# First stretch on six PSUM banks, units 8 to 11 later, units 10 and 11 in split precision, key tails over 128 rows

## The chip, the cores and the metric

The kernel runs on one core of a Trainium2 chip. The metric is the device time of one execution in microseconds (us). Short names: PE is TensorE (PEld its weight loads), DVE is VectorE, ACT is ScalarE, POOL is GpSimd, SP is the queue that issues most DMAs.

## The reference

Three layers follow each other on 2304 tokens: a linear attention with random features, a gated feed-forward layer, and a soft mixture of experts. Cut to what matters:

```python
# attention: q, k, v of shape (4, 8, 576, 64), omega (128, 64)
def phi(x):
    h = einsum('bhsd,md->bhsm', x, omega) - sum(x * x, -1) / 2
    return exp(h - max(h, -1)) / sqrt(128)
q_p, k_p = phi(q * scale), phi(k * scale)
kv = einsum('bhsm,bhsd->bhmd', k_p, v)
num = einsum('bhsm,bhmd->bhsd', q_p, kv)
den = einsum('bhsm,bhm->bhs', q_p, sum(k_p, 2))[..., None] + 1e-06
x = num / den                                   # then (2304, 512)
# gated layer: d_ff 1536
x = (1 / (1 + exp(-(x @ w_gate))) * (x @ w_val)) @ w_out
# soft mixture: 32 slots, 8 experts, softmax over tokens and over slots
logits = x @ phi2
slots = softmax(logits, 0).T @ x
slot_out = [relu(slots[e] @ w1[e]) @ w2[e] for e in range(8)]
out = softmax(logits, 1) @ slot_out
```

## The kernel before, in words

**Attention** works in 16 units, each two heads of one batch entry (`NU`). A unit has the steps `chunk_proj` (five, the products of keys and queries with omega, 9 tiles of 128 rows in all), `chunk_kv` (for each head five accumulating products over the 576 keys: four tiles of 128 rows and a tail of 64), `chunk_qT` (transposes) and `chunk_num` (numerator and denominator, two halves). The tail of 64 key rows shares a tile with the 64 tail rows of the queries: rows 0 to 63 of `HT` are keys, rows 64 to 127 queries. Four units make up one batch entry, and a block of the gated layer needs the four units of its tokens.

**Precision.** A product in plain fp32 is one call that PE runs as two instructions. Units from `N_PROJ` on (projection) and from `N_NUM` on (numerator) use the split form instead: each operand is cut into a high and a low part of type fp32r, and `three` issues three products of one instruction each. The gated layer always uses the split form.

**The gated layer** ("moe" in the code) walks five blocks of up to 512 tokens in 60 steps of one weight tile each: `gate(i)` (12 instructions into bank `ga`), `val(i)` (12 into `va`), `down(i - 1)` (12 into `o0` to `o3`). For the first steps the weights are also decoded from their stored form (`convert`, DVE and ACT work, staged in `g0`) and written to a scratch tensor `wscr`. The groups of steps are: block 0's first six weight tiles, block 1's twelve, block 0's last six, then blocks 2, 3, 4. Block 0's first part is set aside in `part`, and added back by `evac_out(0)` when group 2 (counted from 0) has ended.

**The order** of all instructions is made when the program is built: every step is recorded with a due time, and a list scheduler with its own cost table (`Plan`) writes out one fixed sequence for each engine. `LATE8` and the numbers `start`, `SPAN` set due times; no due time is a time on the chip.

**PSUM** has eight banks: `fl` (two), `ga`, `va`, `o0` to `o3`. While `wide[0]` is true (before the first gated step's due time) attention goes round the list `FLW`; afterwards it has the two `fl` alone.

**SBUF regions** `g0` to `g4` are reused: `split_regions` takes `g0` and `g1` over for the split operands (`XK`, `XQ` are the split keys and queries, `QT`, `KV` the split transposed queries and kv, `obh`, `obl` the split omega). `g0` holds the weight staging before, `g1` holds `part`. At the end all regions take the experts' weights.

Every recorded operation is issued by one line (L379), so the rows of the trace are told apart by tiles: `fl<-g,g` is an attention product into bank `fl`, `ga<-XT,w`, `va<-XT,w` and `o<-gt,w` are the gated layer, `x2T`, `x` and `ws` are weight decoding and staging.

Of the kernel before, what the change touches and what calls it, by code (L numbers as in the profile page):

```python
# [11 lines left out]
F32 = mybir.dt.float32  # L12
F32R = mybir.dt.float32r
# [7 lines left out]
B, H, S, D, M = 4, 8, 576, 64, 128  # L21
NU = B * H // 2
NT = 5
ROWS = [128, 128, 128, 128, 64]
DM, DFF, NTOK = 512, 1536, 2304
NF = DFF // 128

# [27 lines left out]
W1N = 6  # L55
W2N = 3
T0 = -60
N_PROJ = 12
N_NUM = 12
FLOOR = 8  # L60
EARLY = 12.0
SQP = [0, 0, 1, 1, 1, 0, 1, 0]
# [11 lines left out]
SPAN = [88.0, 115.0, 60.0, 120.0, 105.0, 45.0]  # L74
# [307 lines left out]
def body(ctx, tc, nc, qkT, tok, von, omT, wall, phi, w1, w2, ident_d, srep_d, rrep_d, mask_d, out):  # L382
    plan = Plan(nc)
    PE, ACT, DVE, POOL, SP = (Eng(plan, e) for e in ("PE", "ACT", "DVE", "POOL", "SP"))
# [6 lines left out]
    def T(shape, tag, dtype=F32, bufs=1):  # L391
        return plan.tile(sb, shape, dtype, tag, bufs)
# [46 lines left out]
    def region(k, dtype):  # L439
        return T([128, 4096], f"g{k}", dtype)  # L440

    def carve(reg, at, shape):
        n = int(np.prod(shape))
        names = "abcde"[:len(shape)]
        v = reg[:, at:at + n]
        if len(shape) == 1:
            return v
        return v.rearrange(f"p ({' '.join(names)}) -> p {' '.join(names)}",
                           **{c: d for c, d in zip(names, shape)})

    q0, q1 = (region(k, F32) for k in range(2))
    g2, g3, g4 = (region(k, F32) for k in (2, 3, 4))
    QS = [carve(q0, 1024 * k, [1024]) for k in range(4)]
    part = carve(q1, 0, [4, 512])
# [2 lines left out]
    def split_regions():  # L457

        nonlocal QT, KV, XK, XQ, obh, obl
        g0, g1 = (region(k, F32R) for k in range(2))  # L460
        QT = carve(g0, 0, [2, 2, S])
        KV = carve(g0, 2304, [2, 2, 128])
        obh = carve(g0, 2816, [256])
        obl = carve(g0, 3072, [256])
        XK = carve(g1, 0, [2, 640])
        XQ = carve(g1, 1280, [2, 512])
        hi_of(obh, obf, ("DVE",))
        lo_of(obl, obf, obh, ("DVE",))

# [2 lines left out]
    Vs = [carve(g3, 1280 * k, [NT, 2, 128]) for k in range(2)]  # L472
    QTF = carve(g3, 2560, [2, S])
    obf = carve(g3, 3712, [256])
    HK = carve(g4, 0, [4, 2, M])
    HQ = carve(g4, 1024, [4, 2, M])
    HT = carve(g4, 2048, [1, 2, M])
# [10 lines left out]
        return lst[ring[name] % len(lst)]  # L488

    wide = [True]  # L490
    FLW = ["fl", "o0", "o1", "fl", "o2", "o3", "ga", "va"]

    def bank(tag=None):
        if tag is None:
# [11 lines left out]
    def prep_qk(u, kind):  # L506

        if u >= NU:
            return
        if u == N_PROJ and kind == 0:  # L510
            split_regions()
# [37 lines left out]
    def chunk_kv(u):  # L549

        ps = bank()[:, 0:256].rearrange("p (h c) -> p h c", h=2)
        for h in range(2):
            for t in range(NT):
                k = HK[:, t, h, :] if t < 4 else HT[0:64, 0, h, :]
                PE.matmul(ps[:, h, :], k, Vs[u % 2][0:ROWS[t], t, h, :], start=t == 0, stop=t == NT - 1)
        if u < N_NUM:
            ACT.activation(out=KVF, in_=ps, func=AF.Copy, scale=1.0 / M)
            return
        ACT.activation(out=KV[:, 0], in_=ps, func=AF.Copy, scale=1.0 / M)
        DVE.scalar_tensor_tensor(out=KV[:, 1], in0=ps, scalar=1.0 / M, in1=KV[:, 0].bitcast(F32),  # L560
                                 op0=ALU.mult, op1=ALU.subtract)
# [314 lines left out]
    free, spare = [], []  # L876

    def pieces(tag, bufs=1, n=4):
        t = T([128, 1024 * n], tag, F32, bufs)
        return [t[:, 1024 * c:1024 * c + 1024] for c in range(n)]  # L880

# [208 lines left out]
    start = START  # L1090
# [68 lines left out]
    for g, (j, f0, f1) in enumerate(GROUPS):  # L1159
        span = SPAN[g]  # L1160
        for f in range(f0, f1):
            jobs += moe_jobs(i, start + span * (f - f0) / (f1 - f0), span / (f1 - f0))
            i += 1
        units, a0, a1 = {0: (range(4, 8), LATE0 + 5 * LATE1, start + 0.92 * span),
                         1: (range(8, 12), start, start + span + 0.9 * SPAN[2]),
                         3: (range(12, 16), start, start + 0.92 * span)}.get(g, ((), 0, 0))
        att = [c for u in units for c in step_chunks(u)]
        jobs += [(a0 + (a1 - a0) * k / len(att), "att", c) for k, c in enumerate(att)]
        if g > 1:
            m2c = moe2_chunks(GROUPS[g - 1][0])  # L1170
            jobs += [(start + span / (f1 - f0) + span * 0.7 * k / len(m2c), "m2", c) for k, c in enumerate(m2c)]
        if j == NB - 3:
            jobs += [(start + 10.0, "ex", load_w1)]
        if j == NB - 2:
            jobs += [(start + 10.0 + 12 * k, "ex", load_w1) for k in range(6)]
        if j == NB - 1:
            jobs += [(start + 10.0, "ex", load_w1), (start + EARLY, "end", free_early)]
        start += span
# [34 lines left out]
def layout(q, k, v, omega, moe_w_gate, moe_w_val, moe_w_out, moe2_phi, moe2_w1, moe2_w2):  # L1213
    def headsT(x):
        return x.reshape(B, H // 2, 2, S, D).transpose(0, 1, 2, 4, 3).reshape(NU, 128, S)

    def tiles(x, n):
        return x.reshape(NU, 2, n, 128, D).transpose(0, 3, 2, 1, 4)

    def pairs(x):  # L1220
        return x.reshape(NU, 2, S, D)

    kT, qT = headsT(k), headsT(q)
    kp, qp, vp = pairs(k), pairs(q), pairs(v)
    tail = np.concatenate([kp[:, :, 512:], qp[:, :, 512:]], axis=2)
    vtail = tiles(np.concatenate([vp, np.zeros_like(vp[:, :, :64])], axis=2), NT)
    ones = np.ones_like(vtail[:, :, :, 0])

    def up(w):
        return w.reshape(4, 128, NF, 128).transpose(2, 1, 0, 3).reshape(NF, 128, 512)  # L1230

    f32 = np.float32
    p = np.arange(128)
    big = np.finfo(f32).max
    a = {
        "qkT": np.concatenate([kT, qT[:, :, 512:], qT[:, :, :512]], axis=2),
        "tok": np.concatenate([tiles(kp[:, :, :512], 4), tiles(tail, 1), tiles(qp[:, :, :512], 4)], axis=2),
        "von": np.stack([np.concatenate([vtail[:, :, :, 0], ones], axis=3),
                         np.concatenate([ones, vtail[:, :, :, 1]], axis=3)], axis=3),
        "omT": np.concatenate([omega.T, omega.T], axis=0),  # L1240
        "wall": np.stack([up(moe_w_gate), up(moe_w_val), moe_w_out.reshape(NF, 128, DM)], axis=1).view(np.int64),
        "phi": moe2_phi.reshape(4, 128, NSLOT).transpose(1, 0, 2),
        "w1": moe2_w1.reshape(E, 4, 128, F).transpose(0, 2, 1, 3).reshape(E, 128, 4 * F),
        "w2": moe2_w2.reshape(E, 8, 128, 2, DM // 2).transpose(0, 3, 2, 1, 4).reshape(E, 2, 128, 4 * DM),
        "ident": np.eye(128, dtype=f32),
        "srep": (p[:, None] % 32 == np.arange(32)[None, :]).astype(f32),
        "rrep": (p[:, None] % 32 == p[None, :] % 32).astype(f32),
        "mask": np.where((p[:, None] % 32) // SPE == np.arange(E)[None, :], big, f32(0)).astype(f32),
    }
    return {f"in_{n}": np.ascontiguousarray(x) for n, x in a.items()}  # L1250
# [17 lines left out]
```

## Time and profile before

| what | value |
|---|---|
| time, median of 3 runs (lowest, highest) | 712.02 us (711.65, 712.44) |
| the profiled execution's own time | 711.95 us |
| its span, first to last instruction | 710.1 us |
| mean granted TensorE clock | 0.996 |
| PE busy | 690.2 us, 97% of the span |
| PEld, DVE, ACT, POOL busy | 77%, 62%, 61%, 41% |

The profiled execution is 0.07 us below the median, and 1.85 us of its time lie outside the span. A matmul's record is longer than the distance to the next one, since matmuls overlap in the pipeline; what an instruction costs the engine is read from start to start.

### The profile page before, as it was taken

How to read it: one execution, taken by the hardware profiler on the slowest of the kernel's cores; microseconds unless marked ns; L12 is line 12 of the kernel's file. 1: busy time of each engine (PE TensorE's matmuls, PEld its weight loads, DVE VectorE, ACT ScalarE, POOL GpSimd, SP SyncE). 2: the span in 40 equal slices, each digit the busy share in tenths (PEclk: the TensorE clock that was granted, in tenths of full speed). 3: DMA queues.
4: the chain of work that ended last, by engine and by line, in shares of the span. 5: the costliest groups of instructions: out<-in, count | busy, mean ns of one | idle time of the engine just before them, and what ended most of it. 6: DMA issues, size and time to landing. Idle time of an engine off the chain costs nothing.

```text
span 710.1 us, 11979 instructions
## 1 busy us (share of the span) xinstructions
PE 690.2 (97%) x4085; PEld 546.6 (77%) x4085; DVE 441.9 (62%) x1283; ACT 436.1 (61%) x976; POOL 291.2 (41%) x249
## 2 busy tenths in 40 slices
PE   8999999999999999999999999999999999999993
PEld 5667677768788787787788888788888788998662
DVE  4778998788998445463486765546554434775321
ACT  5889898889876644645467675654444445765021
POOL 0355344535445534435364553334444444642000
PEclk9999999999999999999999999999999999999998
DMA  8768777678784334622254234378633327657997
GB/s 296 278 220 285 264 246 262 216 250 283 250 295 138 122 122 136 226 79 68 77 168 137 83 93 161 99 270 298 236 95 94 101 83 247 198 165 208 338 408 263
DMA packets 49980, 139.47 MB, mean 196 GB/s; under 512 B 5504, under 2 KB 10880, under 8 KB 49920
## 3 DMA queue, kind: packets, MB, share of 16 engines
q1 hardware_dynamic: 45312, 121.94, 51.2%
q10 hardware_dynamic: 4608, 16.78, 6.8%
q8 instruction: 32, 0.52, 0.3%
q14 instruction: 28, 0.23, 0.1%
HBM read 124.54 MB, written 14.16 MB: 195 GB/s over the span
## 4 chain that ended last, share of the span: by engine, by line
PE 81%; DVE 3%; issue 1%; ACT 1%; DMA 1%; POOL 0%; POOLq 0%; ACTq 0%; DVEq 0%
PE o L379 23%; PE va L379 21%; PE ga L379 20%; PE fl L379 18%; DVE x2T L379 1%; DVE g L379 1%; DMA wscr<-x 1%; DVE x L379 0%; DVE gt L379 0%; POOL w L379 0%; ACT XT L379 0%; DVE ga_a L379 0%; ACT x2T L379 0%; POOLq L1257 0%; POOL x L379 0%
## 5 line engine op out<-in xcount | busy, mean ns | idle before, releaser
L379 POOL TENSOR_TENSOR w<-ws,w 128x512 fp32r<-128x512 f32 x138 | 182.9, 1326 | 238.0 <-ACT w L379 131.3
L379 PE MATMUL o<-gt,w 128*128 128x512 f32 (+1 forms) x720 | 169.0, 377 | 0.9 <-ACT w L379 0.8
L379 PE MATMUL ga<-XT,w 128*128 128x512 f32 (+1 forms) x720 | 167.1, 376 | 0.0
L379 PE MATMUL va<-XT,w 128*128 128x512 f32 (+1 forms) x720 | 166.5, 375 | 0.0
L379 PEld LDWEIGHTS va<-XT,w 128*128 128x128 f32 x720 | 124.4, 189 | 26.2 <-issue 4.5
L379 PEld LDWEIGHTS o<-gt,w 128*128 128x128 f32 x720 | 123.2, 189 | 27.2 <-issue 4.1
L379 PEld LDWEIGHTS ga<-XT,w 128*128 128x128 f32 x720 | 124.3, 189 | 25.7 <-issue 2.8
L379 ACT ACTIVATE g<-g 128x128 f32<-128x128 f32 (+3 forms) x339 | 119.2, 412 | 21.2 <-DVE g L379 9.5
L379 PE MATMUL fl<-g,g 128*128 128x256 f32 (+3 forms) x668 | 124.7, 345 | 4.1 <-DVE g L379 1.9
L379 PEld LDWEIGHTS fl<-g,g 128*128 128x128 f32 (+2 forms) x668 | 85.9, 178 | 32.4 <-issue 9.0
L379 ACT ACTIVATE w<-ws 128x512 fp32r<-128x512 f32 x107 | 67.3, 629 | 66.3 <-PE o L379 23.6
L379 ACT ACTIVATE ga_a<-ga 128x512 f32<-128x512 f32 (+1 forms) x60 | 33.3, 555 | 79.2 <-PE ga L379 79.1
L379 ACT ACTIVATE ga_a<-ga_a 128x512 f32<-128x512 f32 (+1 forms) x120 | 69.9, 583 | 10.6 <-DVE ga_a L379 9.6
L379 DVE CAST w<-ws 128x512 fp32r<-128x512 f32 x55 | 24.6, 448 | 78.9 <-PE ga L379 55.0
L379 DVE CUSTOM_DVE_ANT_0 g<-fl,g 128x128 f32<-128x128 f32 x252 | 59.0, 285 | 20.2 <-PE fl L379 17.5
L379 DVE SCALAR_TENSOR_TENSOR ga_a<-ga,ga_a 128x512 f32<-128x512 f32 (+1 forms) x60 | 38.1, 635 | 44.4 <-ACT ga_a L379 44.1
L379 DVE TENSOR_TENSOR ga_a<-va,ga_a 128x512 f32<-128x512 f32 (+1 forms) x60 | 38.1, 635 | 19.3 <-ACT ga_a L379 12.4
L379 POOL TENSOR_TENSOR XT<-g,XT 128x64 fp32r<-128x64 f32 (+2 forms) x45 | 29.1, 658 | 49.8 <-ACT XT L379 44.3
L379 ACT ACTIVATE x2T<-g 128x512 f32<-128x512 f32 x72 | 46.2, 667 | 2.6 <-DVE x L379 2.4
L379 DVE TENSOR_SCALAR x2T<-x2T 128x512 f32<-128x512 f32 x72 | 42.4, 597 | 1.1 <-ACT x2T L379 0.9
L379 ACT ACTIVATE ga_a<-ga_a,one_b 128x512 f32<-128x512 f32 (+1 forms) x60 | 40.7, 678 | 1.3
L379 DVE TENSOR_TENSOR gt<-ga_a,gt 128x512 fp32r<-128x512 f32 (+1 forms) x49 | 35.9, 732 | 1.4 <-ACT gt L379 0.4
(197 smaller groups left out, 683.5 us busy)
## 6 DMA issues: line engine op xcount, KB each, us to landing
ws<-wscr SPq DMA_DIRECT2D x42, 512.0 KB, 3.7
ws<-wscr SPq DMA_DIRECT2D x78, 256.0 KB, 2.7
g<-in_wall SPq DMA_DIRECT2D x36, 512.0 KB, 4.9
g<-in_von SPq DMA_DIRECT2D x16, 640.0 KB, 5.5
g<-in_w ACTq DMA_DIRECT2D x20, 512.0 KB, 5.0
wscr<-x SPq DMA_DIRECT2D x36, 256.0 KB, 4.4
g<-in_qkT SPq DMA_DIRECT2D x15, 576.0 KB, 3.8
g<-in_tok SPq DMA_DIRECT2D x15, 576.0 KB, 4.9
```

What stands on the lines that cost most here:

```text
L379: getattr(self.eng[e], method)(*a, **k)
```

## The change

It does five things. (1) `FLW` loses `ga` and `va`: in the first stretch attention goes round six banks. (2) `N_PROJ` and `N_NUM` go from 12 to 10: units 10 and 11 use the split form. (3) For that, the split regions must come earlier: `g1` is cut into two halves, `g1a` for `part` and `g1b` for `XQ`, `obh`, `obl`, and `XK` moves to the end of `g0`. (4) Units 8 to 11 get due times that begin 0.3 of group 1's span later (`LATE8`). (5) The key tail is multiplied over all 128 rows of `HT`; the values' rows 64 to 127 of that tile are zeros already, and the column of ones is zeroed there on the host.

```diff
-ROWS = [128, 128, 128, 128, 64]
...
-N_PROJ = 12
-N_NUM = 12
+N_PROJ = 10
+N_NUM = 10
+LATE8 = 0.3
...
+    def half_region(k, dtype):
+        return T([128, 2048], f"g1{'ab'[k]}", dtype)
...
-    q0, q1 = (region(k, F32) for k in range(2))
+    q0, q1 = region(0, F32), half_region(0, F32)
...
-        g0, g1 = (region(k, F32R) for k in range(2))
+        g0, g1 = region(0, F32R), half_region(1, F32R)
         QT = carve(g0, 0, [2, 2, S])
         KV = carve(g0, 2304, [2, 2, 128])
-        obh = carve(g0, 2816, [256])
-        obl = carve(g0, 3072, [256])
-        XK = carve(g1, 0, [2, 640])
-        XQ = carve(g1, 1280, [2, 512])
+        XK = carve(g0, 2816, [2, 640])
+        XQ = carve(g1, 0, [2, 512])
+        obh = carve(g1, 1024, [256])
+        obl = carve(g1, 1280, [256])
...
-    FLW = ["fl", "o0", "o1", "fl", "o2", "o3", "ga", "va"]
+    FLW = ["fl", "o0", "o1", "fl", "o2", "o3"]
...
-                k = HK[:, t, h, :] if t < 4 else HT[0:64, 0, h, :]
-                PE.matmul(ps[:, h, :], k, Vs[u % 2][0:ROWS[t], t, h, :], start=t == 0, stop=t == NT - 1)
+                k = HK[:, t, h, :] if t < 4 else HT[:, 0, h, :]
+                PE.matmul(ps[:, h, :], k, Vs[u % 2][:, t, h, :], start=t == 0, stop=t == NT - 1)
...
+        if tag == "g1":
+            halves = [half_region(k, F32) for k in range(2)]
+            return [halves[c // 2][:, 1024 * (c % 2):1024 * (c % 2) + 1024] for c in range(n)]
...
-                         1: (range(8, 12), start, start + span + 0.9 * SPAN[2]),
+                         1: (range(8, 12), start + LATE8 * span, start + span + 0.9 * SPAN[2]),
...
+    ones[:, 64:, NT - 1] = 0.0
```

Three places show how the order moves. The first is PE in the first stretch. `fl_...`, `o0_...` with `g3_78,g2_77` are projections (fp32), with `64x288` numerators, with `128x128` kv; `ga_145` is the gated layer's very first product. Before, units 3 and 4's work stands ahead of `ga_145`:

```order
L379 MATMUL fl_142<-g3_78,g2_77 128x256
L379 MATMUL o0_133<-g3_78,g4_79 64x288 x2
L379 MATMUL o1_134<-g3_78,g4_79 64x288
L379 MATMUL fl_132<-g3_78,g4_79 64x288 x2
L379 MATMUL o1_134<-g3_78,g4_79 64x288
L379 MATMUL ga_145<-XT_96,w0_138 128x512 x2
L379 MATMUL fl_135<-g3_78,g4_79 64x288 x2
L379 MATMUL fl_143<-g3_78,g2_77 128x256 x2
L379 MATMUL ga_145<-XT_96,w0_138 128x512 x3
```

In the change the same product begins at unit 1's numerators (`o2_112`, `o3_113`), two units earlier, and stands piece by piece between attention's steps:

```order
L379 MATMUL o1_110<-g3_78,g4_79 64x288 x2
L379 MATMUL o2_112<-g3_78,g4_79 64x288 x2
L379 MATMUL o3_113<-g3_78,g4_79 64x288 x2
L379 MATMUL ga_145<-XT_96,w0_138 128x512
L379 MATMUL o2_118<-g3_78,g2_77 128x256 x2
L379 MATMUL ga_145<-XT_96,w0_138 128x512 x2
L379 MATMUL o0_109<-g3_78,g4_79 64x288 x2
L379 MATMUL o0_115<-g3_78,g4_79 128x128 x2
L379 MATMUL fl_111<-g3_78,g2_77 128x256 x2
```

So the first weight tile's 24 products of gate and value are spread over units 1 to 4, and the same attention instructions stand around them.

The second place is PE at unit 10's first projections, in the change. `fl_316` is unit 9's kv, `ga_313` and `va_317` a gated step of block 1, `fl_320` the split projection (six instructions, two tiles of three); unit 10 had the fp32 form (two instructions, `g3_78,g2_77`) before:

```order
L379 MATMUL o3_260<-gt_293,w2_296 128x512 x3
L379 MATMUL fl_316<-g3_78,g4_79 128x128 x10
L379 MATMUL ga_313<-XT_164,w0_302 128x512 x12
L379 MATMUL fl_320<-g1b_312,g0_311 128x256 x6
L379 MATMUL va_317<-XT_164,w1_306 128x512 x12
```

The split keys (`g0_311`) must be written before `fl_320`, and they lie where the weights were staged.

The third place is PE around the end of block 0 (`XT_96`) and the start of block 2 (`XT_278` before, `XT_299` in the change). Before, unit 12's projections stand after the second gated step of the new block has begun, twelve in a row:

```order
L379 MATMUL ga_461<-XT_278,w0_451 128x512 x9
L379 MATMUL fl_394<-g0_380,g1_381 128x256 x2
L379 MATMUL fl_409<-g0_380,g1_381 128x256 x2
L379 MATMUL ga_461<-XT_278,w0_451 128x512 x3
L379 MATMUL fl_394<-g0_380,g1_381 128x256 x4
L379 MATMUL fl_409<-g0_380,g1_381 128x256 x4
L379 MATMUL va_470<-XT_278,w1_456 128x512 x5
```

In the change all five of unit 12's projection steps stand ahead of block 0's last products, its kv (`fl_452`) stands ahead of block 2's first product, and `fl_453` is unit 13's first projection:

```order
L379 MATMUL o3_395<-gt_434,w2_437 128x512 x3
L379 MATMUL fl_452<-g3_78,g4_79 128x128 x10
L379 MATMUL ga_449<-XT_299,w0_443 128x512 x12
L379 MATMUL fl_453<-g1b_312,g0_311 128x256 x6
L379 MATMUL va_454<-XT_299,w1_447 128x512 x12
```

So unit 12 no longer waits for `part`, which shared a region with the split operands.

## Rows read from the trace of the kernel before

**Rows 1.** The page: busy time of each engine, and the granted clock in tenths.

```profile
PE 690.2 (97%) x4085; PEld 546.6 (77%) x4085; DVE 441.9 (62%) x1283; ACT 436.1 (61%) x976; POOL 291.2 (41%) x249
...
PEclk9999999999999999999999999999999999999998
```

**Rows 2.** Busy time of each engine by stretch; then granted clock, DMA share, GB/s.

```profile
0.00:10.00 10.00, 6.84 (x23) 4.88 (x24) 2.68 (x15) 2.62 (x4) 0.20 (x4) 1.00 0.67 222
10.00:60.00 50.00, 48.17 (x267) 33.66 (x266) 36.89 (x199) 44.29 (x135) 19.06 (x22) 1.00 0.75 272
60.00:160.00 100.00, 99.48 (x493) 72.34 (x492) 87.88 (x272) 88.20 (x213) 42.45 (x39) 1.00 0.74 254
160.00:220.00 60.00, 59.40 (x281) 47.27 (x280) 54.87 (x128) 51.32 (x108) 31.34 (x24) 1.00 0.76 257
220.00:340.00 120.00, 120.00 (x601) 92.82 (x600) 60.35 (x155) 62.51 (x129) 53.80 (x45) 1.00 0.39 127
```

**Rows 3.** PE's waits between 10 and 640 us: us in total, times, longest.

```profile
PE fl L379 <- DVE g L379: 1.8, 4, 0.7
PE o L379 <- DVE g L379: 1.2, 2, 0.7
```

**Rows 4.** PE's instructions in order of time, 11 to 16 us: start, duration, count.

```profile
11.78 1.03 PE L379 MATMUL fl<-g,g 128*128 128x256 f32 x4
12.65 2.97 PE L379 MATMUL o<-g,g 128*128 128x128 f32 x20
15.55 0.66 PE L379 MATMUL va<-ident,g 128*128 128x128 f32 x4
```

**Rows 5.** The same, cut to the first six and eight of unit 3's kv.

```profile
46.93 0.83 PE L379 MATMUL o<-g,g 128*128 128x128 f32 x6
...
46.93 1.05 PE L379 MATMUL o<-g,g 128*128 128x128 f32 x8
```

**Rows 6.** Two gated products after a kv, and two not after one.

```profile
203.11 0.73 PE L379 MATMUL va<-XT,w 128*128 128x512 f32 x2
...
87.26 0.62 PE L379 MATMUL va<-XT,w 128*128 128x512 f32 x2
```

**Rows 7.** PE in order of time: fp32 numerators (128x288) between gated products.

```profile
85.39 0.50 PE L379 MATMUL va<-XT,w 128*128 128x512 f32 x1
85.72 0.40 PE L379 MATMUL o<-gt,w 128*128 128x512 f32 x1
86.05 0.71 PE L379 MATMUL fl<-g,g 128*64 128x288 f32 x4
86.68 0.73 PE L379 MATMUL o<-gt,w 128*128 128x512 f32 x2
```

**Rows 8.** The same for a split unit: projections (128x256) and numerators (128x288).

```profile
444.88 0.52 PE L379 MATMUL fl<-g,g 128*128 128x256 f32 x3
445.23 2.91 PE L379 MATMUL ga<-XT,w 128*128 128x512 f32 x12
447.98 0.95 PE L379 MATMUL fl<-g 128*128 128x288 f32 x6
448.77 2.90 PE L379 MATMUL va<-XT,w 128*128 128x512 f32 x12
```

**Rows 9.** PE and DVE at unit 12's first projections, in order of time.

```profile
359.12 1.21 PE L379 MATMUL fl<-g,g 128*128 128x256 f32 x8 [0.67 <-DVE g L379]
...
358.25 1.42 DVE L379 TENSOR_TENSOR g<-g,g 128x640 fp32r<-128x640 f32 x2
```

**Rows 10.** The splits of a split unit, 340 to 480 us: busy us, mean ns.

```profile
L379 DVE TENSOR_TENSOR g<-fl,g 128x512 fp32r<-128x512 f32 x8 | 5.5, 689 | 2.1 <-ACT g L379 1.9
...
L379 POOL TENSOR_TENSOR g<-g,g 128x640 fp32r<-128x640 f32 x3 | 4.9, 1640 | 5.2 <-ACT g L379 3.2 <-DVE g L379 2.0
```

**Rows 11.** Bank ga between 10 and 21 us: a projection's products and its readers.

```profile
L379 PE MATMUL ga<-g,g x7: 379/379/483, 10.8 to 21.0; 128*128 128x256 f32 x7
L379 DVE CUSTOM_DVE_ANT_0 g<-ga,g x4: 281/287/293, 18.4 to 19.6; 128x128 f32<-128x128 f32 x4
```

## The prediction

> **What bounds the kernel now.** I read the busy shares first, then the stretches, then PE's waits. PE is busy for 97% of the span and no other engine for more than 77%, which is PE's own weight loads [rows 1]. By stretch [rows 2] PE has 48.17 of 50 us from 10 to 60, 99.48 of 100 up to 160 and 120 of 120 from 220 to 340; what idle time it has lies at the two ends. In the whole middle its two longest entries of waiting, both for DVE, come to 3.0 us [rows 3]. So the time is PE's list of instructions, each at its start-to-start price: an instruction that goes away shortens the kernel, as long as the next engine can follow. That engine is ACT: 44.29 of 50 us and 88.20 of 100 in the first two stretches, DVE close to it; behind 220 us both are half idle [rows 2]. The granted clock is 1.00, the level of 2.4 GHz, in each of these stretches, even in the first 10 us with PE busy for 6.84 [rows 1, 2]. So I expect no part of the change to pass through the clock.
>
> **Key tails.** A unit's kv is 20 PE instructions, 16 over 128 rows and 4 over 64. Unit 0's take from 12.65 to 15.55, that is 2.90 us [rows 4]. What one over 128 rows costs shows inside unit 3's kv: the first six take 0.83 us and the first eight 1.05, so 0.11 each [rows 5]. Twenty at 0.11 would be 2.20, so the four short ones carry 0.70 us too much. They also delay what follows: two gated products right behind a kv take 0.73 us, two others 0.62, so 0.11 more [rows 6]. That holds where a gated product follows; elsewhere I have no row, and bound it by 0. A unit saves 0.70 to 0.81; I take the middle, 0.755, and for 16 units **-12.1 us** (11.2 to 13.0). The number of instructions stays, operands and loads are there already, and the extra rows of weights come from the instruction that wrote the tile before, so no wait is added.
>
> **Units 10 and 11 in split form.** Projection, fp32: four instructions from 11.78 to 12.65, 0.2175 each [rows 4]; a unit has 9 tiles of two, 3.92 us. Split: three from 444.88 to 445.23, 0.117 each [rows 8]; 27 make 3.15. Saved: 0.77. Numerator, fp32: four instructions from 86.05 to 86.68, 0.63 us, and around them two gated products from 85.39 to 86.05 take 0.66 [rows 7], where two of a run of twelve take 0.46 (445.23 to 447.98 for twelve, 0.229 each) [rows 8]. So a visit costs 0.20 beside its 0.63 per four. A unit has 16: in two visits of eight 2 x (1.26 + 0.20) = 2.92 us; 2.52 without a visit's price, 3.32 with four visits. Split: six from 447.98 to 448.77, 0.132 each [rows 8], twelve make 1.58. Saved 1.34 (0.94 to 1.74); I take two visits, since the order prints eight of them together at most places. Both units: 2 x 2.11 = **-4.2 us** (3.4 to 5.0).
>
> What the split adds lies on other engines: a cast and a subtraction for keys, for queries, for the transposed queries and for kv. The rows for such work say 0.69 us each on DVE and 1.64 on POOL [rows 10]; at about ten a unit it is some 10 us a unit over three engines, 20 in all. Units 10 and 11 are worked between about 220 and 340 us, where DVE is busy for 60 of 120, ACT for 63 and POOL for 54 [rows 2]: 183 idle engine-microseconds. I cost it at nothing. Without that cover (between 60 and 160 us) a part of the 20 would come back through ACT.
>
> **Moved regions.** Splitting omega needs two DVE instructions; the order puts them at the start, where DVE has 7.3 of 10 us idle [rows 2]: nothing. Unit 12's projections lose a wait: PE stood still for 0.67 us there, released by DVE, whose split of the keys (358.25, two of them in 1.42 us) had come late behind the block's end [rows 9]. In the change they stand well ahead of it: **-0.7 us** (0 at worst, where the wait moves to another place).
>
> **The first stretch.** The gated products of weight tile 0 can fill PE's idle time from 10 to 60 us, which is 1.8 us in all [rows 2]: at most 1.8 to win. Against this stands ACT. Units 0 to 7 give up 8 x 0.755 = 6.0 us of PE work inside 10 to 160 us; ACT's work there stays 132.5 of 150 us, so its idle time would go from 17.5 to 11.5 us. PE and ACT hand banks to each other in fixed order and cannot both run without pause. The loss lies between nothing and all 6.0; since a third of ACT's idle time is asked for, I take a third: **+2.0 us**. The later due times of units 8 to 11 take attention out of 160 to 220 us and put it behind; PE's total stays, and I cost it at nothing. It is covered by the gated products themselves; if DVE (54.87 of 60 there [rows 2]) could not keep up with steps that follow each other more closely, it would cost PE a part of DVE's missing 5 us.
>
> **Sum**, against the profiled execution: 711.95 - 12.1 - 4.2 - 0.7 + 2.0 = 696.95, so **697.0 us**. The median of the three runs, 712.02, is 0.07 above that execution, which I neglect.
>
> **Rivals.**
>
> *ACT takes all that the early tails give.* Place: 10 to 160 us. For it: ACT at 88% in both stretches [rows 2], and its order asks for the same work before the first gated steps as before. Against: it would need ACT to keep every bit of its 17.5 idle us. Then the time is 711.95 - 12.1 - 4.2 - 0.7 + 6.0 = 701.0 us.
>
> *A new wait at unit 10's first split projection.* The split keys lie where weights are staged, so they wait for the last decoded weight, and the order gives PE twelve gated products (2.75 us at 0.229) between unit 9's kv and the projection. POOL's share of the split is 1.64 us [rows 10]. If the last decoding is late by two such instructions, PE stands still for about 3 us and everything behind it is 3 us later: 700 us. Against: POOL is busy for only 54 of 120 us there [rows 2].
>
> *The idle time is filled and ACT follows.* 711.95 - 12.1 - 4.2 - 0.7 - 1.8 = 693.2 us. For it: the first gated products stand where PE waited.
>
> *The tail's price is not that of its 64 rows.* If 0.70 us came from the tail tile's place and not from its shape, it would stay: 711.95 - 4.2 - 0.7 + 2.0 = 709.1. Against: the instructions over 128 rows beside it, with the same operand tiles, cost 0.11 [rows 5].
>
> *Six banks are too few; slower than before.* A unit takes 13 banks (5 projections, kv, 3 transposes, 4 numerators), four units 52 from about 10 to 55 us, one in 0.87 us. A ring of eight comes round in 6.9 us, one of six in 5.2. Bank ga was written from 10.8 us on and its last reader began at 19.6 [rows 11]: 9 us, longer than either. Without the 2.0 for ACT the gain is 17.0 us; from a wait of 0.33 us a bank, 52 x 0.33 = 17.2, all of it is gone, and above that the kernel is slower: at 0.4 us 711.95 - 17.0 + 20.8 = 715.8 us. Against: with eight banks PE waited 3.0 us for DVE in the whole middle [rows 3], and the long hold is one of a bank that was filled early, not one that PE then waited for. The Trainium skill, Perfetto Trace Analysis, Matmul Optimizations, asks that all eight PSUM banks be used so that as many instructions as possible can overlap; by that rule the change goes the wrong way in the first stretch. The two banks are not left empty here but go to tile 0, so I give this rival little.
>
> **How the numbers follow.** Main case 0.66, between 694.5 and 699.5. ACT takes all 0.15. Wait at unit 10 0.08. Idle time filled 0.06. Tail's price elsewhere 0.02. Too few banks 0.03, of which 0.01 within 0.2% of before. About 0.2%, 1.4 us, is what this measurement can tell from no change. Range: downwards every bound together, 711.95 - 13.0 - 5.0 - 1.8 - 0.7 = 691.4, of which I take 692; upwards 711.95 - 11.2 - 3.4 + 6.0 = 703.4, of which I take 703. It leaves out the last two cases and the edges. Faster 0.97, same 0.01, slower 0.02.
>
> **What would show it.** A unit's kv at 2.2 us and the product behind it at its usual price: the tails. PE's instructions over 64 rows gone but for the transposes. Projections of units 10 and 11 at 0.117, numerators at 0.132, with no PE wait in front of the first. No wait of 0.67 us at unit 12. PE's idle time from 10 to 160 us, 2.35 before, at about 4.4 in the main case; above 8 means that ACT is the bound there. The prediction is wrong if that idle time grows past 8 us, or if PE waits for the split keys.

## The result, and the profile after

The changed kernel took 703.9 us, the median of four runs (702.4 to 704.3), where the kernel before took 712.2 in runs beside them. The measured ratio is 0.9865, with a 95% interval of 0.9846 to 0.9884; the quotient of the two medians, 0.988, lies just inside it. The profiled execution took 703.83 us with a span of 702.0, which is 8.1 us less than that of before. The prediction was 697.0, so 15 us had been forecast, and 8 (medians) to 10 us (ratio) of it came. The median lies 0.9 us above the top of the range given; by the ratio, 711.95 x 0.9865 = 702.3, the time lies 0.7 below it.

What was forecast of PE's list is there. Two places of the profile after, PE in order of time: unit 0's kv with what follows it, and unit 10's first split projection between gated products.

```profile
12.94 2.47 PE L379 MATMUL o<-g,g 128*128 128x128 f32 x20 [0.49 <-DMA g<-in_von]
15.24 0.60 PE L379 MATMUL o<-ident,g 128*128 128x128 f32 x4
...
227.84 0.88 PE L379 MATMUL fl<-g1b,g 128*128 128x256 f32 x6
228.55 2.91 PE L379 MATMUL va<-XT,w 128*128 128x512 f32 x12
```

From start to start that kv takes 2.30 us, against 2.90 in [rows 4]; over the eleven kvs whose twenty instructions stand together the median is 2.15, so a unit saves 0.75. The six split instructions take 0.71, or 0.118 each, as in [rows 8], and nothing waits in front of them.

The loss shows by stretch (busy us of each engine, then the granted clock) and in PE's waits between 10 and 640 us (us in total, times, longest):

```profile
10.00:60.00 50.00, 46.16 (x275) 33.79 (x275) 39.18 (x201) 45.03 (x134) 19.72 (x21) 1.00 0.84 293
60.00:160.00 100.00, 97.74 (x492) 72.28 (x490) 88.53 (x275) 88.33 (x210) 48.89 (x43) 0.98 0.75 249
160.00:220.00 60.00, 56.49 (x259) 44.33 (x258) 57.26 (x108) 49.44 (x97) 28.71 (x21) 1.00 0.70 240
220.00:340.00 120.00, 119.41 (x659) 98.22 (x658) 69.22 (x224) 76.62 (x169) 58.60 (x51) 1.00 0.44 143
```

```profile
PE fl L379 <- DVE g L379: 4.7, 9, 1.3
PE ga L379 <- DVE ga_a L379: 2.6, 2, 1.9
PE va L379 <- DVE ga_a L379: 1.4, 1, 1.4
PE o L379 <- ACT g L379: 0.9, 1, 0.9
```

Beside [rows 2], PE is busy for 2.0 us less of the stretch from 10 to 60, 1.7 less up to 160, and 2.9 less from 160 to 220. The waits shown come to 9.6 us, against the 3.0 of [rows 3]; 8.7 of them have DVE as their releaser, not ACT.

To see where, I priced each of PE's instructions in either order by the median start-to-start time that its kind, between the same kinds of neighbours, has in the kernel before. By these prices the changed list is 16.3 us shorter, which is the forecast's 12.1 + 4.2. This is an estimate: where the kinds are told apart a little differently it comes to 18.0, and the loss below to 9.9 instead of 8.2. What each kernel takes above its priced list:

| up to the first product of | before | after | lost in this stretch |
|---|---|---|---|
| step 2 (79 us before) | 9.6 us | 14.6 us | 5.0 |
| step 8 (175 us) | 12.0 | 17.0 | 0.0 |
| step 12 (220 us) | 13.1 | 20.5 | 2.4 |
| step 59 (645 us) | 20.4 | 28.6 | 0.8 |

So by this pricing 8.2 us are lost, 5.0 in the first 80 us and 2.4 between 175 and 220. The largest single place is at 64.7 us. PE, DVE and POOL there, in order of time (an entry in brackets is the idle time before, and what ended it), and below them the stretches around it:

```profile
66.63 1.93 PE L379 MATMUL ga<-XT,w 128*128 128x512 f32 x5 [1.90 <-DVE ga_a L379]
...
64.21 1.77 DVE L379 CUSTOM_DVE_ANT_0 x<-x2T 128x1024 uint16<-128x1024 uint16 x1
65.90 0.68 DVE L379 SCALAR_TENSOR_TENSOR ga_a<-ga,ga_a 128x512 f32<-128x512 f32 x1
...
63.65 1.78 POOL L379 TENSOR_TENSOR w<-x,w 128x512 fp32r<-128x512 f32 x1 [2.37 <-ACT w L379]
```

```profile
64.00:66.00 2.00, 0.73 (x4) 0.27 (x2) 2.00 (x3) 1.53 (x5) 1.43 (x1) 1.00 0.78 221
66.00:68.00 2.00, 1.37 (x5) 1.08 (x6) 2.00 (x11) 1.93 (x5) 1.23 (x1) 0.83 1.05 388
68.00:70.00 2.00, 2.00 (x8) 1.68 (x7) 1.55 (x4) 2.00 (x6) 1.04 (x2) 0.50 0.90 330
70.00:75.00 5.00, 5.00 (x24) 3.91 (x23) 3.19 (x13) 3.44 (x10) 1.80 (x3) 0.93 0.78 242
```

Step 1's gate needs bank ga, which DVE's instruction at 65.90 frees; ahead of it on DVE stands an addition of the weight decode. Behind the wait the granted clock is 0.83, 0.50 and 0.93, a mean between its levels of 1.2 and 2.4 GHz: 0.7 + 2.0 + 0.7 = 3.4 us at the lower one, which cost 1.7 us. With the 1.9 us of the wait this one place is worth up to 3.6.

### The profile page after: what moved, and what is told of

Its sections match the earlier page's. It is cut to its first block, busy times and chain, and to the rows that moved or that the text cites. A ratio compares the mean times of both kernels' runs of the same rounds, so it can differ in the third digit from the quotient of the medians.

```text
span 702.0 us, 12020 instructions
## 1 busy us (share of the span) xinstructions
PE 676.4 (96%) x4095; PEld 544.6 (78%) x4095; DVE 446.4 (64%) x1297; ACT 443.9 (63%) x984; POOL 296.4 (42%) x251
## 4 chain that ended last, share of the span: by engine, by line
PE 66%; DVE 5%; DMA 2%; issue 2%; ACT 2%; POOL 0%; POOLq 0%; SPq 0%; ACTq 0%; DVEq 0%
PE o L379 19%; PE ga L379 18%; PE va L379 17%; PE fl L379 11%; DVE x2T L379 2%; DMA ws<-wscr 1%; DMA wscr<-x 1%; DVE x L379 1%; DVE g L379 1%; DVE ga_a L379 1%; ACT ga_a L379 0%; ACT x2T L379 0%; ACT XT L379 0%; ACT g L379 0%; POOL w L379 0%
## 5 line engine op out<-in xcount | busy, mean ns | idle before, releaser
L379 POOL TENSOR_TENSOR w<-ws,w 128x512 fp32r<-128x512 f32 x140 | 184.9, 1321 | 240.5 <-ACT w L379 134.4
L379 PE MATMUL ga<-XT,w 128*128 128x512 f32 (+1 forms) x720 | 170.0, 378 | 2.6 <-DVE ga_a L379 2.6
L379 PE MATMUL va<-XT,w 128*128 128x512 f32 (+1 forms) x720 | 166.2, 375 | 1.4 <-DVE ga_a L379 1.4
L379 PE MATMUL o<-gt,w 128*128 128x512 f32 (+1 forms) x720 | 165.3, 374 | 0.9 <-ACT w L379 0.8
L379 PEld LDWEIGHTS ga<-XT,w 128*128 128x128 f32 x720 | 123.8, 189 | 30.8 <-issue 5.7
L379 PEld LDWEIGHTS va<-XT,w 128*128 128x128 f32 x720 | 124.1, 189 | 26.8 <-issue 3.7
L379 PEld LDWEIGHTS o<-gt,w 128*128 128x128 f32 x720 | 123.6, 189 | 24.1 <-issue 2.2
L379 ACT ACTIVATE g<-g 128x128 f32<-128x128 f32 (+4 forms) x342 | 122.2, 413 | 19.1 <-DVE g L379 14.0
L379 ACT ACTIVATE w<-ws 128x512 fp32r<-128x512 f32 x106 | 66.5, 628 | 60.0 <-PE o L379 18.9
L379 PE MATMUL fl<-g,g 128*128 128x128 f32 (+2 forms) x514 | 88.3, 342 | 3.3 <-DVE g L379 2.7
L379 PEld LDWEIGHTS fl<-g,g 128*128 128x128 f32 (+1 forms) x514 | 63.2, 180 | 20.5 <-issue 8.5
L379 ACT ACTIVATE ga_a<-ga 128x512 f32<-128x512 f32 (+1 forms) x60 | 33.3, 554 | 70.7 <-PE ga L379 70.7
L379 ACT ACTIVATE ga_a<-ga_a 128x512 f32<-128x512 f32 (+1 forms) x120 | 70.0, 583 | 10.9 <-DVE ga_a L379 10.0
L379 DVE CUSTOM_DVE_ANT_0 g<-fl,g 128x128 f32<-128x128 f32 x242 | 57.3, 285 | 18.6 <-PE fl L379 18.0
L379 DVE CAST w<-ws 128x512 fp32r<-128x512 f32 x56 | 24.2, 431 | 70.0 <-PE ga L379 40.0
L379 DVE SCALAR_TENSOR_TENSOR ga_a<-ga,ga_a 128x512 f32<-128x512 f32 (+1 forms) x60 | 38.1, 635 | 46.4 <-ACT ga_a L379 46.1
L379 POOL TENSOR_TENSOR XT<-g,XT 128x64 fp32r<-128x64 f32 (+2 forms) x46 | 30.6, 678 | 54.0 <-ACT XT L379 51.4
L379 ACT ACTIVATE x2T<-g 128x512 f32<-128x512 f32 x72 | 45.9, 666 | 6.3 <-DVE x L379 6.2
L379 DVE TENSOR_TENSOR ga_a<-va,ga_a 128x512 f32<-128x512 f32 (+1 forms) x60 | 38.0, 634 | 15.8 <-ACT ga_a L379 10.9
L379 ACT ACTIVATE ga_a<-ga_a,one_b 128x512 f32<-128x512 f32 (+1 forms) x60 | 40.7, 678 | 1.3
L379 DVE TENSOR_SCALAR x2T<-x2T 128x512 f32<-128x512 f32 (+1 forms) x72 | 39.8, 563 | 1.8 <-ACT x2T L379 1.7
L379 DVE TENSOR_TENSOR gt<-ga_a,gt 128x512 fp32r<-128x512 f32 (+1 forms) x49 | 37.3, 762 | 1.0 <-ACT gt L379 0.2
```

What stands on the lines that cost most here:

```text
L379: getattr(self.eng[e], method)(*a, **k)
```

## The experiments

Ratios are against the kernel before, run beside each on the same chip; its medians there were 712.4 to 713.8. The brackets are 95% intervals. An edit that adds lines moves the issuing line's number (L378, L380, L392 for L379).

### Undo parts of the change

Theory L was that the six banks and the later due times had brought the new waits.

**Tails alone**, on the kernel before:

```diff
-                k = HK[:, t, h, :] if t < 4 else HT[0:64, 0, h, :]
-                PE.matmul(ps[:, h, :], k, Vs[u % 2][0:ROWS[t], t, h, :], ...)
+                k = HK[:, t, h, :] if t < 4 else HT[:, 0, h, :]
+                PE.matmul(ps[:, h, :], k, Vs[u % 2][:, t, h, :], ...)
...
+    ones[:, 64:, NT - 1] = 0.0
```

> The kernel before with the key tails over 128 rows and nothing else. Theory L (PE's list is priced right, and the gain of 8 instead of 15 us is lost to waits that the six banks and the later due times bring): PE's own list is 12.1 us shorter, no new wait, so 700 us, 699 to 701.5. Theory A (ACT and DVE are the bound from 10 to 160 us and take what the early tails give, whatever the banks are): at most the tails behind 160 us count, 706 us, 704 to 708. If the price of the tail belongs to its place and not to its 64 rows: 712.

Measured: 712.5 us, ratio 0.9994 [0.9978, 1.0009]. Nothing at all, although a kv takes 2.15 us (median) in its trace. Neither theory had this; the third forecast has the time, but not the reason, since the price of the 64 rows did go.

**Due times undone, eight banks again, and both**, on the changed kernel:

```diff
-LATE8 = 0.3
+LATE8 = 0.0
```

> The changed kernel with units 8 to 11 due from the start of their stretch again (LATE8 = 0), six banks as changed. PE's order is the changed kernel's up to about 65 us. Theory L: the four waits of PE for DVE between 159 and 208 us (0.72, 1.41, 0.77, 0.60 us) come from gated steps that follow each other without attention between them, and go: about 700.5 us, 699.5 to 702, and DVE's busy share from 160 to 220 us falls from 95% to about 91%. The wait of 1.9 us at 64.7 us stays. Theory A, or the due times cost nothing: 703.9, within 1 us.

```diff
-    FLW = ["fl", "o0", "o1", "fl", "o2", "o3"]
+    FLW = ["fl", "o0", "o1", "fl", "o2", "o3", "ga", "va"]
```

> The changed kernel with banks ga and va given back to the first stretch's ring of eight; due times as changed. Theory L: the excess of about 5 us that PE gathers up to 81 us (a wait of 1.9 us at 64.7 us for the gate, the half clock behind it, and some of half a microsecond each) goes for the most part: about 700 us, 699 to 702. Theory A: the waits move but their sum up to 160 us stays, 703.9 within 1 us. If the two banks spared PE idle time at the start (its excess up to the first gated step fell by 1.6 us): 705 to 706.

> The changed kernel with the ring of eight and LATE8 = 0: tails, split units 10 and 11 and the moved regions are left of the change. Theory L: both new groups of waits go, about 697 us, 696 to 699, the predicted 697.0 without its 2.0 for the first stretch being 695. Theory A: 702 to 704, since PE's shorter list runs into ACT and DVE with any number of banks.

| changed kernel with | LATE8 = 0 | LATE8 = 0.3 |
|---|---|---|
| ring of eight | 708.6 us, 0.9933 [0.9914, 0.9952] | 711.1 us, 0.9968 [0.9954, 0.9982] |
| ring of six | 706.5 us, 0.9901 [0.9880, 0.9922] | 0.9865, the change itself |

Theory L falls: to undo either part makes the kernel slower, not faster. The six banks are worth 0.3% with units 8 to 11 early and 1.0% with them late; the later due times cost 0.35% with eight banks and gain 0.36% with six. The differences of 0.3% are each hardly larger than their own uncertainty (0.2 to 0.3%), but that the worth of one part changes with the other is clear of it (0.7%, give or take 0.4). Neither part has a price of its own. The times that theory A gave for these runs were missed too (704 to 708 us for the tails alone, 702 to 705 for the others); its idea, that ACT and DVE take what the early tails give whatever the order, was still open.

### Instruction and order taken apart

The planner reads a matmul's cost from its operand. Tails of 64 rows stand in its table at 0.416 us, others of this size at 0.222:

```python
return (0.416 if ins[0].ap[0][1] == 64 else max(0.222, n / 600.0)), False
```

So the tail edit, which touches no due time, also told the planner that 32 matmuls had become cheaper by 0.194 us each, 6.2 us in all, and it wrote other sequences for all engines. Theory D has the elementwise engines, DVE above all, set the pace up to 220 us, so that any shorter list of PE turns into waits; theory O has the new sequences lose what the tails gain. Two kernels hold one of the two fixed. **New tails, old order**: the kernel with the tails alone, with

```diff
+                if t == 4:
+                    plan.tails.append(k)
...
-            return (0.416 if ins[0].ap[0][1] == 64 else max(0.222, n / 600.0)), False
+            return (0.416 if any(ins[0] is x for x in self.tails) else max(0.222, n / 600.0)), False
```

> The kernel before with the tails over 128 rows, but the planner goes on costing a tail as it did, so that every engine has the order of the kernel before, row for row. The tails alone, with the order that the planner makes of the new cost, gave nothing (712.5). Theory D (up to 220 us the elementwise engines, DVE above all, set the pace, and PE's shorter list turns into waits): only the four units behind 340 us save time, 3.0 us, and of the other twelve (9.1 us) at most a third: 706 to 709. Theory O (DVE could follow, but the planner's new order is a bad one): 700, 699 to 701.5. If the tail's price is not that of its 64 rows: 712.

**Old tails, new order**: the kernel before, with

```diff
+                if t == 4:
+                    plan.tails.append(k)
...
-            return (0.416 if ins[0].ap[0][1] == 64 else max(0.222, n / 600.0)), False
+            return (0.416 if ins[0].ap[0][1] == 64 and not any(ins[0] is x for x in self.tails) else max(0.222, n / 600.0)), False
```

> The kernel before with its tails over 64 rows, but with every engine in the order of the run with the tails alone (the planner is told the new cost, the instruction stays). It closes a square: old order and old tails 712.2, old order and new tails 11 us less, new order and new tails 0 to 0.4 us less. Theory O1 (the new order has waits of its own, which come on top of PE's list whatever that holds): about 11 us above the kernel before, 720 to 724, ratio 1.012 to 1.017. Theory O2 (in the new order the elementwise engines set the pace up to 220 us, so that PE's longer tails would hide in the waits and only the four late units' 3 us count): 713 to 716, ratio 1.002 to 1.005.

| | old order | new order | what the order costs |
|---|---|---|---|
| tails of 64 rows | 1 | 724.5 us, 1.0167 [1.0153, 1.0181] | +1.7%, 11.9 us |
| tails of 128 rows | 703.8 us, 0.9843 [0.9819, 0.9868] | 712.5 us, 0.9994 [0.9978, 1.0009] | +1.5%, 10.8 us |
| what the tails save | 1.6%, 11.2 us | 1.7%, 12.3 us | |

In the traces PE, DVE, ACT and POOL run the same sequence, instruction for instruction, within each column of this table. The microseconds are those of the ratios. The two effects add up within the error, as theory O1 has it: the two savings differ by 1.1 us, and the intervals leave about 2.3 open. The tails save 11 to 12 us in either order (12.1 had been forecast), and the order that the new cost makes takes 11 to 12 us back. Theories A and D, by which DVE and ACT could not follow a shorter list, fall: in the old order with new tails DVE and ACT are busier up to 160 us than before, and PE is idle there for 3.2 us, against 2.35; by the ratio the kernel takes 701.0 us (0.9843 of 712.2). The stretches of new tails in the old order:

```profile
10.00:60.00 50.00, 47.92 (x288) 35.67 (x287) 39.08 (x209) 46.84 (x139) 20.37 (x23) 1.00 0.81 289
60.00:160.00 100.00, 98.86 (x502) 73.12 (x500) 90.62 (x275) 90.91 (x218) 43.11 (x39) 1.00 0.78 266
160.00:220.00 60.00, 57.86 (x268) 45.77 (x267) 53.95 (x118) 47.47 (x101) 32.00 (x25) 0.97 0.72 240
```

and in the new order:

```profile
10.00:60.00 50.00, 46.70 (x260) 31.45 (x260) 33.20 (x188) 42.28 (x127) 16.77 (x19) 1.00 0.75 265
60.00:160.00 100.00, 98.51 (x500) 71.27 (x499) 94.31 (x279) 85.72 (x207) 53.00 (x48) 1.00 0.75 250
160.00:220.00 60.00, 57.24 (x272) 45.50 (x271) 56.84 (x136) 51.20 (x108) 26.41 (x20) 1.00 0.77 267
```

In the new order DVE does 5.9 us less work from 10 to 60 us, and by then has done 6 of the decode's 72 single-input instructions instead of 10; it catches up from 60 to 160 us, where POOL too has 9.9 us more to do. That waits belong to the order shows in three of PE's that the old order does not have (with new tails its longest wait for ACT between 10 and 640 us is 0.2 us, and none is for DVE's x), first with new tails and then with old ones (PE in order of time, the same three instructions):

```profile
42.09 0.70 PE L378 MATMUL ga<-g,g 128*64 128x288 f32 x2 [0.69 <-ACT g L378]
...
199.05 1.13 PE L378 MATMUL fl<-g,g 128*128 128x256 f32 x4 [1.94 <-ACT g L378]
...
395.87 1.38 PE L378 MATMUL fl<-g,g 128*128 128x128 f32 x10 [1.14 <-DVE x L378]
```

```profile
44.21 0.70 PE L380 MATMUL ga<-g,g 128*64 128x288 f32 x2 [0.69 <-ACT g L380]
...
204.56 1.13 PE L380 MATMUL fl<-g,g 128*128 128x256 f32 x4 [1.92 <-ACT g L380]
...
406.01 2.21 PE L380 MATMUL fl<-g,g 128*128 128x128 f32 x14 [1.15 <-DVE x L380]
```

They are equal to 0.02 us, though PE's list differs by 12 us. The three come to 3.8 us, but waits are not the whole price of the order. PE over the whole of the four profiled runs:

| tails, order | span | PE busy | PE idle |
|---|---|---|---|
| 64 rows, old | 710.1 us | 690.2 us | 19.9 us |
| 64 rows, new | 724.0 | 698.9 | 25.1 |
| 128 rows, old | 703.3 | 681.2 | 22.1 |
| 128 rows, new | 709.5 | 684.9 | 24.6 |

In these single runs the new order costs 13.9 us with old tails and 6.2 with new ones. Of that 5.2 and 2.5 us are idle time; 8.7 and 3.7, the larger part, lie in PE's busy time, though the instructions are the same ones. Part of that is the lower clock, which some of these runs met and others did not (0.97 on average from 160 to 220 us in two of the four). Another part is shorter visits, whose price the prediction worked out, but for units 10 and 11 alone: the 192 numerators in fp32 are done in 37 visits instead of 32, and take 31.0 us from start to start instead of 29.0 and 29.2. What the rest is made of is not shown.

### Is DVE the bound? Less work for it, in the same order

On the tails alone, without the decode's 36 clamps:

```diff
         for _, _, (e, method, a, k) in self.schedule():
+            if method == "tensor_scalar" and k["scalar1"] is W_LO:
+                continue
```

> The tails alone again, in the very order of that run (712.5), but the 36 clamps of the weight decode are not issued: one instruction of DVE on 128x512 in each decoded weight tile, 24.9 us of DVE's busy time up to 225 us. The clamp of the weights' range is what is left out. Theory D: PE gets back the time for which it waited on DVE: 703 to 706, with DVE's busy share from 60 to 220 us well below the 94% of that run. Theory O: the waits come from what stands ahead of what, for ACT and POOL as much as for DVE: 711 to 712.5.

Measured: 709.4 us, 0.9930 [0.9911, 0.9949], between the two forecasts. The clamps had taken 24.9 us; DVE's busy time falls by 18.1 us in all, and the kernel gains 4.6 us. So DVE's share is real: the wait of 1.94 us at 199.05 above shrinks to 0.20. But most of the 11 stay with the order as it is; the 1.1 us at the place of 395.87, behind the decode, are there unchanged.

### The six banks by themselves

On the kernel before:

```diff
-    FLW = ["fl", "o0", "o1", "fl", "o2", "o3", "ga", "va"]
+    FLW = ["fl", "o0", "o1", "fl", "o2", "o3"]
```

> The kernel before with the ring of six banks in the first stretch and nothing else. Theory D: six banks pay because tile 0's gated steps, and with them DVE's and ACT's work on them, start 25 us earlier and fill those engines' idle time in the first 60 us; PE's list is not shorter here and PE had 3.7 us of idle time between 10 and 220 us, so at most 3: 709 to 712. Rival S (six banks are worth the 7.2 us by themselves that they made of 711.1 to 703.9): 705. Rival P (the prediction's rival that six are too few): above 713.

Measured: 716.1 us, 1.0030 [1.0016, 1.0043], so slower by 0.3%. On the unchanged list the prediction's rival, that six are too few, has the right sign. The Trainium skill, Perfetto Trace Analysis, Matmul Optimizations, has the rule that all eight banks be used; this run agrees with it in sign. With new tails and split units the same edit gained 0.3 to 1.0%. Again the worth is that of the order which comes out.

### One place mended

On the changed kernel, step 0's gate at 64.7 us: two instructions of ACT and one of DVE are moved ahead, once the order is made.

```diff
+        exp, ln, dve = (order[k] for k in g[1:])
+        rest = [x for k, x in enumerate(order) if k not in g[1:]]
+        at = rest.index(order[g[0]]) + 1
+        rest[at:at] = [exp, ln]
+        at = rest.index(order[before])
+        rest[at:at] = [dve]
```

> The changed kernel with three instructions moved by one or two places: in step 0's gate ACT's exponential and logarithm stand right behind the absolute value, ahead of a weight conversion and a key function, and DVE's instruction that frees bank ga stands ahead of an addition of the decode that took 1.77 us. All other engines' orders stay. Theory C (the wait of 1.9 us of PE at 64.7 us and the half clock behind it, 3.4 us long, cost 1.9 + 1.7): PE waits there less than 0.5 us, the clock stays at 1.00, and the time is 701 to 702. Theory D: what PE gains there it waits for later, since DVE has as much to do before 220 us as before: 703 to 704.

Measured: 703.3 us, 0.9846 [0.9824, 0.9868], with a span of the profiled run of 700.2, 1.8 less than the changed kernel's. The intervals of the two kernels overlap, and the run does not decide between the forecasts: its median lies in theory D's range, and by its ratio (0.9846 of 712.2 is 701.2) it lies in theory C's. What happened at the place is plain, though. PE and then DVE:

```profile
64.99 0.70 PE L392 MATMUL ga<-XT,w 128*128 128x512 f32 x2 [0.55 <-ACT g L392]
66.64 0.96 PE L392 MATMUL ga<-XT,w 128*128 128x512 f32 x3 [0.94 <-POOL w L392]
...
64.16 0.69 DVE L392 SCALAR_TENSOR_TENSOR ga_a<-ga,ga_a 128x512 f32<-128x512 f32 x1 [0.17 <-ACT ga_a L392]
64.77 0.68 DVE L392 CUSTOM_DVE_ANT_0 x<-x2T 128x1024 uint16<-128x1024 uint16 x1
```

The wait of 1.90 for the bank is gone, but two others took its place, 1.49 us together: the next late thing was the weights' low part, two gated products later. The clock, though, stayed at 1.00 there. It fell behind the one long wait, and not behind these two shorter ones with work between them. The 1.8 us that the profiled run is shorter are about the 0.4 us less of waiting there and the 1.7 us of the half clock; that this gain holds for the medians too (0.6 us) is not shown.

### The split, and the parts put together in the old order

**Split alone**: the changed kernel with eight banks, LATE8 = 0 and tails over 64 rows. **Tails and split in the old cost**: the same with the tails over 128 rows and the first edit of the square above. All engines have the same order in these two.

> The kernel before with units 10 and 11 split and the regions moved, tails over 64 rows, ring of eight, LATE8 = 0; every engine has the same order as in the run above it. The predicted term is -4.2 us (3.4 to 5.0), and -0.7 for the wait at unit 12: 707.3 where the kernel before takes 712.2, ratio 0.993 (0.992 to 0.995). If the split's casts and subtractions are not covered: 710 to 712.

Measured: 710.95 us, 0.9967 [0.9955, 0.9979], by the ratio a gain of 2.4 us and not 4.9. PE's priced list is 3.6 us shorter (by the same estimate) and the wait at unit 12 is gone, but there are two new ones, at unit 10's first split projections (PE in order of time):

```profile
218.83 0.51 PE L380 MATMUL fl<-g1b,g 128*128 128x256 f32 x2 [0.72 <-ACT g L380]
...
222.88 0.86 PE L380 MATMUL fl<-g1b,g 128*128 128x256 f32 x5 [0.76 <-DVE g L380]
```

> Tails over 128 rows, units 10 and 11 split and the moved regions, with the ring of eight and LATE8 = 0, and the planner costing a tail as it did before (all engines have the order of the kernel before up to about 180 us). With the planner's new cost the same parts took 708.6. Theory O (PE's terms are right, -11.2 measured for the tails and about -4 for the split, and what is missing is lost to the order that the new cost makes): 697 to 699 where the kernel before takes 712.2, a ratio of 0.979 to 0.981. Theory D (elementwise engines follow only so far, and the split's extra work uses that up): 702 to 704.

Measured: 699.0 us, 0.9812 [0.9790, 0.9834], the best of all these kernels and 0.5% better than the change. It leaves out two parts of the change, the six banks and the later due times, and keeps a cost in the planner's table that is wrong for the tail. This is what theory O gave. By its ratio it gains 13.4 us of the 16.3 that the forecast's two terms make; its trace has two waits at the same place as with the split alone, 0.72 and 0.78 us, which are about half of what is missing.

**The whole change with the old cost** (that one edit on the changed kernel):

> The changed kernel, whole, with the planner costing a tail as it did before. Theory O in its strong form (the new cost of the tail makes bad orders): 696 to 699, ratio about 0.979. In its weak form (every new order gathers its own waits, the six banks and the later due times bring a new order in any case): no better than the changed kernel, 702 to 706, ratio 0.986 to 0.991.

Measured: 708.5 us, 0.9932 [0.9912, 0.9952], slower than the change itself and than both forecasts. So the old cost is no better as such. Its waits in front of the gates alone, where the changed kernel has 2.6 us:

```profile
PE ga L380 <- DVE ga_a L380: 4.6, 3, 1.8
```

The strong form of theory O falls and the weak one stands in its sign: each order has losses of its own, and old and new cost, six and eight banks, early and late units each make another order.

## Why the prediction was half right, point by point

- **The bound, and the tails at -12.1.** Right. A kv went from 2.90 to 2.15 us, and the two columns of the square measure 11.2 and 12.3. The rival that the price does not belong to the 64 rows is out.
- **The split at -4.2, the wait at unit 12 at -0.7.** PE's price of a projection was right (0.118), and the wait is gone. What the split gave in the whole time was 4.3 us between the tails alone and tails with split in the new cost (0.9994 to 0.9933), 2.2 in the old one (0.9843 to 0.9812) and 2.4 with old tails. The first two are uncertain by about 2 us; the last, by 0.9, is below the forecast. The rival of a new wait at unit 10's first split projection came true in the old order, 1.5 us, and not in the changed kernel.
- **"So no wait is added" of the tails.** This is the step that failed, and with it the premise that an instruction which goes away shortens the kernel as long as the next engine can follow. It counted instructions, operands and loads, and left out that the tail's shape is an input of the planner. With the tails alone the order that came of it costs 11 to 12 us on top of the list. In the whole change, where the other parts change the order as well, what is lost on top of the list is about 8 us.
- **The first stretch at +2.0, sized from ACT's idle time.** Mis-sized, and the reason given was not the one. PE's idle time from 10 to 160 us was 6.1 us, between the 4.4 of the main case and the 8 that would have meant ACT; with 1.7 us of half clock the loss there is about 5. ACT was not the bound: in the old order it worked 46.84 of 50 us and 90.91 of 100, and PE was idle for 0.9 us more than before. The releaser of most of the new waits is DVE. The top of the range was worked out from ACT taking all 6.0 us; that the time came out close to it, for another reason, is luck.
- **The later due times at nothing.** Wrong as an argument: they cost 2.5 us with eight banks and gain 2.6 with six, each uncertain by about 2. The forecast's condition, that DVE might not keep up from 160 to 220, did come about (57.26 of 60 us busy), and 2.4 us were lost from 175 to 220; but with the units early again and six banks the whole was slower still.
- **No part through the clock.** Wrong by 1.7 us in the profiled run, behind one wait of 1.9. Nor does the 1.00 of the first 10 us tell everything: the first four projections take 1.13 us in the kernel before (at 4.30) and 2.08 with the tails alone (at 4.51), with 1.00 in both views; why is not shown.
- **Six banks too few.** Right in sign on the old list (+0.3%), wrong on the new one.

In sum, the forecast's -16.3 for PE's list stands; what came on top of the list was about 8.2 us, where the forecast had +2.0 for the first stretch and -0.7 for the wait at unit 12, 1.3 in all.

What stays open is why one order loses so much more than another. The later decode in the new order is seen in the trace, and the kernel without the clamps got 4.6 us back, but no single rule of the planner was shown to be the cause, and the loss inside PE's busy time is only in part accounted for.

## What to carry to other kernels

Where a planner writes the order, an edit has two effects, the instructions and the order, and they can be of one size and opposite sign: for the tails alone about -12 and +11 us. Look whether the edit changes anything that the planner reads, a shape among it, and measure the two apart by holding the order fixed; an edit that then pays can be kept with the order that it had. A part that is tested alone, or undone alone, then tells little about what it is worth in the whole.

## What the hardware showed

- DVE instructions stretch while POOL works. All 27 additions of the decode on DVE, in the changed kernel (shortest, median and longest in ns, then first and last start):

```profile
L379 DVE CUSTOM_DVE_ANT_0 x<-x2T x27: 674/682/1786, 28.0 to 215.2; 128x1024 uint16<-128x1024 uint16 x27
```

In ten of the 27 an instruction of POOL was already running when DVE's began: each of the ten ended 0.55 to 0.60 us after POOL's did, and took 0.68 to 1.79 us, according to when POOL ended. The other 17 took 0.67 to 0.69, whether POOL started during them or not. The one at 64.21 took 1.77 us; POOL had worked since 63.65 and ended at 65.43, 0.55 us before it. With the gate mended that addition started before POOL's next instruction and took 0.68. The Trainium skill, Trainium Architecture — The Big Picture, What this means for kernel authors, says that on the engines' side only the port pair that DVE and GpSimd share contends, as an exclusive lock; the trace agrees. So part of why an order is slow can be which of the two comes first.
- A wait of about 2 us was followed by the lower clock in some runs (1.90 us at 64.7 in the changed kernel; 1.92 at 202.6 with old tails in the new order) and not in others: the same wait of 1.94 us with new tails left the clock at 1.00. The stretches that follow the last two waits, in this order:

```profile
206.00:208.00 2.00, 2.00 (x6) 1.60 (x5) 1.97 (x11) 2.00 (x7) 1.81 (x3) 0.51 0.93 331
...
200.00:202.00 2.00, 2.00 (x10) 1.63 (x9) 1.97 (x11) 2.00 (x7) 2.00 (x2) 1.00 1.01 337
```
